# The two matrix products of a feed-forward block take turns on TensorE, one matmul of each

## The chip, the cores and the metric

One NeuronCore of a Trainium2 chip runs the whole program. The metric is the device time of one execution in microseconds (us); less is better. TensorE (PE in the profile) does the matrix products and has a separate row for its weight loads (PEld). VectorE (DVE), ScalarE (ACT) and GpSimd (POOL) do the elementwise work, and SyncE (SP) issues all DMA transfers.

## The reference

Attention over a window of keys and over block summaries comes first, then a feed-forward block with a squared ReLU. Four batches, 8 heads, 768 positions, head size 64; the feed-forward block has 3072 tokens, width 512 and 2048 hidden units.

```python
a = softmax(concat([where(abs(i - j) < 16, s * q @ k.T, -1e9), s * q @ k_sum.T + log(32)]))
x = (a @ concat([v, v_sum])).transpose(0, 2, 1, 3).reshape(3072, 512)
h = x @ w_in                  # 3072 x 2048
g = np.maximum(h, 0.0) ** 2
return (g @ w_out).astype(np.float32)
```

## The kernel before

**Tiling.** The tokens are cut into 48 groups of 64 (`g`), and eight groups make a unit (`u`, 0 to 5) of 512 tokens. The 2048 hidden units are cut into 16 slices (`f`) of 128. A pair (u, f) is an item, and there are 96 items in order. Each product is done in three terms: a high part and a low part of each operand, without low times low (`xh`, `xl` of the input; `gh`, `gl` of the hidden values; two halves of each weight tile `w0_f` and `w1_f`).

**The first product of an item** (task `FI`, function `hidden`, line 676) adds 12 matmuls of 128x512 into one tile `h` of PSUM, of which there are two. ScalarE and VectorE then make `r` (ReLU, task `RL`, line 684), its square (`SQ`, line 690 on VectorE, 686 on ScalarE for the first two units), `gh` (`GH`, line 692) and `gl` (`GL`, line 695).

**The second product of an item** (task `FO`, function `outer`, line 702) is another 12 matmuls, three into each of four tiles `o` that add up over the 16 items of a unit. After the last item of a unit, `put` copies the four tiles (`PC`, line 727 on ScalarE and 729 on VectorE) and stores them (`PS`).

**Attention for later units** runs between: per group, scores (`s`, line 462), on VectorE, ScalarE and GpSimd the softmax, a transposition through memory (`turn`, lines 560 and 566), and the product with the values (`x`, line 578). In a new batch, VectorE also takes maxima over the keys (`kb`, line 310) and sums of the values (`part`, line 389); in the first two batches the means of the values are matmuls (`vps`, line 355). The weights are unpacked once, during unit 0 (`convert`, lines 621 to 644), over a tile `t` from a pool of four that the value loads share.

**The order** is not written by hand. Each step is a task with a cost, a due time and its predecessors. `Plan.order` runs a list scheduler over all engines and emits the tasks in the order in which they start there. The engines then run their queues in that order, each instruction waiting only for its own data. The due time of a second product is 2.5 steps (`LAG` = 2) behind that of its first:

```python
due += (LAG + 0.5) * STEP
todo = [(t, i) for t in range(NTT) for i in range(3)]
if first or last:
    pieces = [[x for x in todo if x[0] == t] for t in range(NTT)]
else:
    pieces = [sorted(todo, key=lambda x: x[1] == 2)]
```

Of the kernel before, what the change touches and what calls it, by code (L numbers as in the profile page):

```python
# [10 lines left out]
F32 = mybir.dt.float32  # L11
F32R = mybir.dt.float32r
U32 = mybir.dt.uint32
I64 = mybir.dt.int64
AF = mybir.ActivationFunctionType
ALU = mybir.AluOpType
# [4 lines left out]
P = 128  # L21
# [5 lines left out]
SQ = 32  # L27
NSQ = P // SQ
UG = 8
TU = UG * TQ  # L30
# [2 lines left out]
NV = 3  # L33
NPE = 16
LAG = 2


REBIAS = 2.0**-112
# [55 lines left out]
class Plan:  # L94
# [8 lines left out]
    def add(self, name, engine, cost, emit, key, after=(), take=(), use=(), size=0, begin=0.0, behind=None):  # L103
        t = Task(name, engine, cost, emit, key, [a for a in after if a is not None], list(take), list(use), size, begin)
        t.behind = behind
        t.index = len(self.tasks)
        self.tasks.append(t)
        for b in t.take + t.use:
            b.users.append(t)
        return t  # L110
# [63 lines left out]
def attention_then_relu2_ffn(  # L174
# [9 lines left out]
    nc = tc.nc  # L184
    B, H, S, D = v.shape
    NT, DM = out.shape
    NF = wW.shape[1]
# [5 lines left out]
    NU = NG // UG  # L193
    KT = DM // P
    NTT = TU // P
# [6 lines left out]
    add = plan.add  # L202
# [3 lines left out]
    def buf(tag, n, shape, dtype, name, pool=None, fixed=False):  # L206
        if tag not in kinds:
            tiles = [cst.tile(list(shape), dtype, name=f"{tag}{i}") for i in range(n)] if fixed else None
            kinds[tag] = Slots(pool or sb, tag, n, tiles)
        assert kinds[tag].n == n  # L210
        return Buf(kinds[tag], shape, dtype, name)

    def o_buf(name, cols=512):
        return buf("o", 4, (P, cols), F32, name, ps)

    def h_buf(name, cols=512):
        return buf("h", 2, (P, cols), F32, name, ps)
# [12 lines left out]
    items = [(u, f) for u in range(NU) for f in range(NF)]  # L230
    T0, SLOW, STEP = 35.0, 7.1, 6.5
    unit_at = [T0 + NF * (SLOW * min(u, 1) + STEP * max(u - 1, 0)) for u in range(NU + 1)]
    at_item = {(u, f): unit_at[u] + f * (STEP if u else SLOW) for u, f in items}
# [18 lines left out]
    xh = cst.tile([P, KT, RING * TQ], F32R, name="xh")  # L252
    xl = cst.tile([P, KT, RING * TQ], F32R, name="xl")
# [45 lines left out]
    t_S, t_KC, t_T, t_V, t_XL = {}, {}, {}, {}, {}  # L299
    t_K = {}  # L300

    def batch_k(b):
        key = wanted(b * NW) - 30 if b else -90
        prev = [t_S[b * NW - 1]] if b else []

        def load(p):
            nc.sync.dma_start(out=kb[:, p, NB:], in_=kT[b, p * P : (p + 1) * P, :])

        def top(p):
            nc.vector.tensor_reduce(  # L310
                out=kb[:, p, :NB], in_=kb[:, p, NB:].rearrange("p (j r) -> p j r", r=BLOCK), op=ALU.max, axis=AX.X
            )

        t_K[b] = []
        for p in range(NPAIR):
            t = add(f"KL{b}_{p}", "SP", 0.45, lambda p=p: load(p), key + 0.1 * p, prev, size=4 * P * S)
            t_K[b].append(add(f"KM{b}_{p}", "DVE", 0.945, lambda p=p: top(p), key + 0.1 * p, [t]))
# [282 lines left out]
    t_W = {}  # L600
    w_bufs = {}

    def convert(f, n):
# [3 lines left out]

        due = at_item[0, f] + (LAG * STEP if n else 0)

# [46 lines left out]
        t_W[n, f] = [t6, t7]  # L656


    t_FI = {}

    def ffn(u, f, o, done):

        first, last = f == 0, f == NF - 1
        due = at_item[u, f]
        c0 = u % 2 * TU
        wi, wo = ([Part(w_bufs[n, f], 0, DM), Part(w_bufs[n, f], DM, 2 * DM)] for n in range(2))
        h = h_buf(f"h{u}_{f}")
        r, gh, gl = (
            buf(tag, n, (P, TU), dt, f"{tag}{u}_{f}") for tag, n, dt in (("r", 2, F32), ("gh", 3, F32R), ("gl", 3, F32R))
        )  # L670

        def hidden():
            i = 0
            for k in range(KT):
                for lhs, rhs in ((wi[0], xh), (wi[1], xh), (wi[0], xl)):
                    nc.tensor.matmul(  # L676
                        h.tile, lhsT=lhs.tile[:, k * P : (k + 1) * P], rhs=rhs[:, k, c0 : c0 + TU],
                        start=(i == 0), stop=(i == 3 * KT - 1),
                    )
                    i += 1  # L680

        deps = t_W[0, f] + [t_XL[g] for g in range(u * UG, (u + 1) * UG)] + list(t_FI.values())[-1:]
        t1 = t_FI[u, f] = add(f"FI{u}_{f}", "PE", 2.79, hidden, due, deps, take=[h])
        t2 = add(f"RL{u}_{f}", "ACT", 0.62, lambda: nc.scalar.activation(r.tile, h.tile, AF.Relu), due + 3, [t1], take=[r], use=[h])  # L684
        if u < 2:
            t3 = add(f"SQ{u}_{f}", "ACT", 0.62, lambda: nc.scalar.activation(r.tile, r.tile, AF.Square), due + 4, [t2], use=[r])
        else:
            t3 = add(
                f"SQ{u}_{f}", "DVE", 0.7,
                lambda: nc.vector.tensor_tensor(out=r.tile, in0=r.tile, in1=r.tile, op=ALU.mult), due + 4, [t2], use=[r],  # L690
            )
        t4 = add(f"GH{u}_{f}", "ACT", 0.62, lambda: nc.scalar.copy(out=gh.tile, in_=r.tile), due + 5, [t3], take=[gh], use=[r])  # L692
        t5 = add(
            f"GL{u}_{f}", "DVE", 0.7,
            lambda: nc.vector.tensor_tensor(out=gl.tile, in0=r.tile, in1=gh.tile.bitcast(F32), op=ALU.subtract),  # L695
            due + 6, [t4], take=[gl], use=[r, gh],
        )
        terms = ((gh, wo[0]), (gh, wo[1]), (gl, wo[0]))

        def outer(todo):  # L700
            for t, i in todo:
                nc.tensor.matmul(  # L702
                    o[t].tile, lhsT=terms[i][0].tile[:, t * P : (t + 1) * P], rhs=terms[i][1].tile,
                    start=(first and i == 0), stop=(last and i == 2),
                )

        due += (LAG + 0.5) * STEP
        todo = [(t, i) for t in range(NTT) for i in range(3)]
        if first or last:
            pieces = [[x for x in todo if x[0] == t] for t in range(NTT)]  # L710
        else:
            pieces = [sorted(todo, key=lambda x: x[1] == 2)]
        for i, piece in enumerate(pieces):
            t6 = add(
                f"FO{u}_{f}_{i}", "PE", 0.2325 * len(piece), lambda piece=piece: outer(piece), due + 0.1 * i,
                [t4, t5] + t_W[1, f] + done[-1:],
                take=[o[i]] if first else [], use=[gh, gl] + ([] if first else [o[i]] if last else o),
            )
            done.append(t6)
            if last:  # L720
                put(u, i, o[i], t6, due + 0.1 * i)

    def put(u, i, o, t, due):
        rows = slice(u * TU + i * P, u * TU + (i + 1) * P)
        x = buf("half", 4, (P, DM), F32, f"os{u}_{i}")
        if i % 2:
            t2 = add(f"PC{u}_{i}", "ACT", 0.62, lambda: nc.scalar.copy(out=x.tile, in_=o.tile), due + 0.6, [t], take=[x], use=[o])
        else:
            t2 = add(f"PC{u}_{i}", "DVE", 0.7, lambda: nc.vector.tensor_copy(out=x.tile, in_=o.tile), due + 0.6, [t], take=[x], use=[o])
        add(f"PS{u}_{i}", "SP", 0.45, lambda: nc.sync.dma_start(out=out[rows, :], in_=x.tile), due + 1, [t2], use=[x], size=4 * P * DM)  # L730
# [6 lines left out]
    def groups(n):  # L737
        nonlocal done_g
        while done_g < n:
            g = done_g  # L740
            b, w = divmod(g, NW)
            if b and not w:
                batch_k(b)
                (batch_v_pe if b < 2 else batch_v)(b)
            attention(g)
            done_g += 1

    groups(UG)
    for f in range(NF):
        for n in range(2):  # L750
            convert(f, n)
    done = []
    for u in range(NU):
        groups((u + 1) * UG)
        o = [o_buf(f"o{u}_{t}") for t in range(NTT)]
        for f in range(NF):
            ffn(u, f, o, done)

    for t in plan.tasks:
        if t.name in FIRST:  # L760
# [51 lines left out]
```

## Time and profile before

| what | value |
|---|---|
| median of 3 runs | 666.93 us (666.03 to 668.0) |
| profiled execution | 667.02 us, span 665.3 us |
| TensorE matmul busy | 643.5 us, 97% of the span, 3544 instructions |
| VectorE / ScalarE / GpSimd busy | 51% / 42% / 13% |
| DMA | 75.61 MB, mean 114 GB/s |

The span is the time between the first and the last instruction of the profiled execution. A row with one start time and a count stands for instructions that follow each other; the recorded time of one matmul is longer than the distance to the next, since they overlap. What a matmul costs in a stream is therefore read from the distance between starts.

### The profile page before, as it was taken

To read this page: it belongs to the slowest core of one execution; us is meant where nothing else is said; L and a number is where in the kernel's file an instruction comes from. 1 tells how busy PE (TensorE), PEld (TensorE's weight loads), DVE (VectorE), ACT (ScalarE), POOL (GpSimd) and SP (SyncE) were. 2 spreads that over 40 slices of the span, in tenths; PEclk is the share of its full clock that TensorE was granted. 3 is DMA by queue.
4 is the path that set the end of the run, shared out by engine and by line. 5 is a ranking of instruction groups with operands and counts; after the bars stand their busy time and mean duration, and the time that the engine had idled before them with its cause. 6 is when DMAs were issued, how large, how long until landed. Compare 5 with 4: busy or idle time off the path is not lost.

```text
span 665.3 us, 9719 instructions
## 1 busy us (share of the span) xinstructions
PE 643.5 (97%) x3544; PEld 511.2 (77%) x3544; DVE 340.3 (51%) x612; ACT 278.6 (42%) x751; POOL 83.6 (13%) x140
## 2 busy tenths in 40 slices
PE   4979999999999999999999999899999999999997
PEld 3557668878887878787888877778878888888886
DVE  4698879985433375644434586443553342322222
ACT  2688559775534443433323432233343242222221
POOL 3741001100201001101110200110110010000000
PEclk9979999999999999999999999999999999999999
DMA  9955657502523381633141482322352311000001
GB/s 308 323 196 180 237 213 245 187 24 75 157 76 80 78 256 42 182 88 76 49 115 45 150 254 75 101 73 75 97 149 56 91 34 33 32 33 1 0 1 63
DMA packets 50215, 75.61 MB, mean 114 GB/s; under 512 B 6440, under 2 KB 22824, under 8 KB 50168
## 3 DMA queue, kind: packets, MB, share of 16 engines
q1 hardware_dynamic: 50168, 75.00, 36.8%
q8 instruction: 28, 0.46, 0.3%
q14 instruction: 19, 0.16, 0.1%
HBM read 59.75 MB, written 14.68 MB: 112 GB/s over the span
## 4 chain that ended last, share of the span: by engine, by line
PE 86%; DVE 4%; SPq 4%; DMA 3%; issue 1%; POOL 1%; ACT 0%; DVEq 0%; ACTq 0%; POOLq 0%
PE h L676 38%; PE o L702 37%; PE s L462 6%; PE x L578 4%; PE vps L355 2%; SPq L560 1%; DMA vr<-v 1%; DVE part L389 1%; DMA fv_lent<-vS 1%; PE t L532 1%; SPq L440 1%; SPq L413 1%; POOL qv_lent L443 0%; DMA a<-turn 0%; DMA out<-os 0%
## 5 line engine op out<-in xcount | busy, mean ns | idle before, releaser
L676 PE MATMUL h<-xh,w 128*128 128x512 f32 x768 | 245.7, 401 | 0.5 <-ACT xh L588 0.5
L702 PE MATMUL o<-w,gh 128*128 128x512 f32 x768 | 203.9, 400 | 0.0
L676 PEld LDWEIGHTS h<-xh,w 128*128 128x128 f32 x768 | 143.2, 189 | 35.0 <-issue 0.8
L702 PEld LDWEIGHTS o<-w,gh 128*128 128x128 f32 x768 | 139.8, 188 | 32.3 <-issue 1.7
L676 PE MATMUL h<-xl,w 128*128 128x512 f32 x384 | 152.8, 398 | 0.3 <-DVE xl L591 0.3
L684 ACT ACTIVATE r<-h 128x512 f32<-128x512 f32 x96 | 57.2, 595 | 183.6 <-PE h L676 159.9
L695 DVE TENSOR_TENSOR gl<-r,gh 128x512 fp32r<-128x512 f32 x96 | 69.1, 720 | 85.4 <-PE o L702 53.8
L702 PE MATMUL o<-w,gl 128*128 128x512 f32 x384 | 109.2, 391 | 0.0
L690 DVE TENSOR_TENSOR r<-r 128x512 f32<-128x512 f32 x64 | 44.8, 700 | 96.8 <-ACT r L684 95.7
L692 ACT CAST gh<-r 128x512 fp32r<-128x512 f32 x96 | 59.6, 621 | 77.7 <-PE o L702 48.9
L676 PEld LDWEIGHTS h<-xl,w 128*128 128x128 f32 x384 | 72.7, 189 | 18.5 <-DVE xl L591 1.0
L702 PEld LDWEIGHTS o<-w,gl 128*128 128x128 f32 x384 | 72.1, 188 | 15.8
L503 ACT ACTIVATE p<-p,nm 128x118 f32<-128x118 f32 x160 | 61.1, 384 | 49.0 <-DVE nm L494 49.0
L519 POOL TENSOR_TENSOR p<-p,nm 128x472 f32<-128x472 f32 x40 | 45.1, 1128 | 184.4 <-DVE nm L513 106.9
L474 POOL COPY kb<-kb 128x96 f32<-128x96 f32 x44 | 17.1, 389 | 275.8 <-PE s L462 271.7
L462 PEld LDWEIGHTS s<-kb,q 128*128 128x128 f32 x320 | 41.6, 191 | 5.2 <-POOL p L483 1.2
L462 PE MATMUL s<-kb,q 128*128 128x118 f32 x320 | 42.1, 274 | 1.0 <-POOL p L483 1.0
L484 DVE SCALAR_TENSOR_TENSOR p<-s,mask 128x472 f32<-128x472 f32 x40 | 25.8, 645 | 26.0 <-PE s L462 25.5
L578 PEld LDWEIGHTS x<-a,v 118*64 118x64 f32 x640 | 22.0, 137 | 17.6 <-issue 12.4
L549 DVE STREAM_TRANSPOSE a<-p 128x512 f32<-128x512 f32 x32 | 22.7, 708 | 19.6 <-POOL p L519 19.6
L512 DVE TENSOR_SCALAR nm<-nm 128x4 f32<-128x4 f32 x48 | 8.9, 185 | 44.9 <-ACT p L503 43.5
L578 PE MATMUL x<-a,v 118*64 118x64 f32 x640 | 27.4, 228 | 3.5 <-DMA a<-turn 2.9
(55 smaller groups left out, 423.3 us busy)
## 6 DMA issues: line engine op xcount, KB each, us to landing
raw<-wW SPq DMA_DIRECT2D x32, 512.0 KB
q<-qW SPq DMA_DIRECT2D x40, 256.0 KB
turn<-a SPq DMA_DIRECT2D x128, 64.0 KB
a<-turn SPq DMA_DIRECT2D x32, 256.0 KB
v<-vS SPq DMA_DIRECT2D x36, 192.0 KB
kb<-kT SPq DMA_DIRECT2D x16, 384.0 KB
out<-os SPq DMA_DIRECT2D x24, 256.0 KB
vr<-v SPq DMA_DIRECT2D x16, 192.0 KB
```

The costliest lines, as they stand in the source:

```text
L462: nc.tensor.matmul(s_ps.tile[:, p * KEYS : (p + 1) * KEYS], lhsT=q.tile[:, p, :], rhs=kb[:, p, k0 : k0 + KEYS], start=True, stop=True,)
L484: nc.vector.scalar_tensor_tensor(out=pr.tile[:, :, :KEYS], in0=s_ps.tile.rearrange("p (n k) -> p n k", k=KEYS), scalar=1.0 / math.sqrt(D), ...
L503: nc.scalar.activation(x, x, AF.Exp, bias=nm.tile[:, p : p + 1], scale=1.0, accum_out=nm.tile[:, NPAIR + p : NPAIR + p + 1],)
L519: nc.gpsimd.tensor_tensor(out=x, in0=x, in1=nm.tile[:, 2 * NPAIR :].unsqueeze(2).broadcast_to([P, NPAIR, KEYS]), op=ALU.mult)
L549: nc.vector.transpose(out=a.tile.rearrange("p (j n r) -> p j n r", j=NSQ, n=NPAIR), in_=pr.tile.rearrange("p n (j c) -> p j n c", c=SQ),)
L578: nc.tensor.matmul(x_ps.tile[h % 2 * D : (h % 2 + 1) * D, h // 2 * TQ : (h // 2 + 1) * TQ], lhsT=vv.tile[:KEYS, h * D : (h + 1) * D], rhs= ...
L676: nc.tensor.matmul(h.tile, lhsT=lhs.tile[:, k * P : (k + 1) * P], rhs=rhs[:, k, c0 : c0 + TU], start=(i == 0), stop=(i == 3 * KT - 1),)
L684: t2 = add(f"RL{u}_{f}", "ACT", 0.62, lambda: nc.scalar.activation(r.tile, h.tile, AF.Relu), due + 3, [t1], take=[r], use=[h])
L690: lambda: nc.vector.tensor_tensor(out=r.tile, in0=r.tile, in1=r.tile, op=ALU.mult), due + 4, [t2], use=[r],
L692: t4 = add(f"GH{u}_{f}", "ACT", 0.62, lambda: nc.scalar.copy(out=gh.tile, in_=r.tile), due + 5, [t3], take=[gh], use=[r])
L695: lambda: nc.vector.tensor_tensor(out=gl.tile, in0=r.tile, in1=gh.tile.bitcast(F32), op=ALU.subtract),
L702: nc.tensor.matmul(o[t].tile, lhsT=terms[i][0].tile[:, t * P : (t + 1) * P], rhs=terms[i][1].tile, start=(first and i == 0), stop=(last an ...
```

## The change

The first and second product are planned together, in one function `ffn(n, done)` for item number n. It cuts the first product of item n into two halves of six matmuls, and also the second product of item n - 2. From item 10 on (`APART`), each half is one task `FM` that emits one matmul of the first product, one of the second, and so on. Ahead of item 10 the halves are tasks of their own. The second product's matmuls are sorted by term, so that neighbours write different `o` tiles; in the first and the last item of a unit they are sorted by pairs of tiles. The elementwise tasks and `put` stay, with due times shifted by 0.4 of a step, and `put` is called for two tiles at a time.

```diff
+APART = 10
...
+            def hidden(k, i):
+                lhs, rhs = ((wi[0], xh), (wi[1], xh), (wi[0], xl))[i]
+                nc.tensor.matmul(
+                    h.tile, lhsT=lhs.tile[:, k * P : (k + 1) * P], rhs=rhs[:, k, c0 : c0 + TU],
+                    start=(k == i == 0), stop=(k == KT - 1 and i == 2),
+                )
+
+            for j in range(3 * KT):
+                parts[2 * j // (3 * KT)][0].append(lambda j=j: hidden(*divmod(j, 3)))
...
+        if n >= LAG:
+            u2, f2 = items[n - LAG]
...
+            todo = [(t, i) for t in range(NTT) for i in range(3)]
+            if first or last:
+                todo.sort(key=lambda x: (x[0] // 2, x[1]))
+            else:
+                todo.sort(key=lambda x: x[1])
+            for j, x in enumerate(todo):
+                parts[2 * j // len(todo)][1].append(lambda x=x: outer(*x))
...
+        def run(*lists):
+            for j in range(max(map(len, lists))):
+                for x in lists:
+                    if j < len(x):
+                        x[j]()
...
+            if n < APART:
+                if first_p:
+                    t = add(f"FI{name}", "PE", 0.2325 * len(first_p), lambda x=first_p: run(x), d, deps[0], take=takes_h, use=uses_h, behind=latest(0))
+                    done[0].append(t)
+                if second_p:
+                    t = add(f"FO{name}", "PE", 0.2325 * len(second_p), lambda x=second_p: run(x), d + 0.5 * STEP, made + t_W[1, f2], take=begun, use=uses[j], behind=latest(1))
+                    done[1].append(t)
+            else:
+                t = add(
+                    f"FM{name}", "PE", 0.2325 * (len(first_p) + len(second_p)), lambda x=first_p, y=second_p: run(x, y), d,
+                    deps[j] + (done[1][-1:] if n == APART else []), take=takes_h + begun, use=uses_h + uses[j],
+                    behind=latest(0),
+                )
+                done[0].append(t)
+                done[1].append(t)
+            if n >= LAG and last:
+                for i in (2 * j, 2 * j + 1):
+                    put(u2, i, o[i], done[1][-1], d + 0.5 * STEP + 0.1 * i)
...
+            due += 0.4 * STEP
...
+    for n in range(len(items) + LAG):
+        if n < len(items) and items[n][1] == 0:
+            groups((items[n][0] + 1) * UG)
+        ffn(n, done)
```

On TensorE, in the middle of unit 2, the queue before has the first product of slice 7 in one piece and then the second product of slice 5 (`h2_7` is the tile of unit 2, slice 7; `o2_0` is output tile 0 of unit 2):

```order
L676 MATMUL h2_7_2897<-xh_68,w0_7_995 128x512 x2
L676 MATMUL h2_7_2897<-xl_69,w0_7_995 128x512
L578 MATMUL x27_2915<-a27_2781,v1_74 64x64 x8
L702 MATMUL o2_0_2687<-w1_5_964,gh2_5_2847 128x512 x2
L702 MATMUL o2_1_2720<-w1_5_964,gh2_5_2847 128x512 x2
L702 MATMUL o2_2_2732<-w1_5_964,gh2_5_2847 128x512 x2
L702 MATMUL o2_3_2749<-w1_5_964,gh2_5_2847 128x512 x2
L702 MATMUL o2_0_2687<-w1_5_964,gl2_5_2849 128x512
L702 MATMUL o2_1_2720<-w1_5_964,gl2_5_2849 128x512
```

At the same place the changed kernel has one matmul of each in turn:

```order
L675 MATMUL h2_7_2883<-xh_68,w0_7_987 128x512
L689 MATMUL o2_0_2607<-w1_5_959,gh2_5_2858 128x512
L675 MATMUL h2_7_2883<-xh_68,w0_7_987 128x512
L689 MATMUL o2_1_2608<-w1_5_959,gh2_5_2858 128x512
L675 MATMUL h2_7_2883<-xl_69,w0_7_987 128x512
L689 MATMUL o2_2_2637<-w1_5_959,gh2_5_2858 128x512
L675 MATMUL h2_7_2883<-xh_68,w0_7_987 128x512
L689 MATMUL o2_3_2638<-w1_5_959,gh2_5_2858 128x512
```

The matmuls are the same; each now has neighbours that write another tile, stream another operand and use other weights.

On ScalarE, in unit 0, the queue before unpacks the weight tile `w1_4` (`t1_4` is its first step) ahead of the exponentials of groups 10 and 11 (`nm10`, `nm11`):

```order
L621 ACTIVATE t1_4_750<-raw1_4_652 128x512
L503 ACTIVATE p0_76,nm10_747<-p0_76,nm10_747 128x118 x4
L692 CAST gh0_3_777<-r0_3_726 128x512
L684 ACTIVATE r0_4_795<-h0_4_754 128x512
L686 ACTIVATE r0_4_795<-r0_4_795 128x512
L641 CAST w1_3_802<-t1_3_691 128x512
L692 CAST gh0_4_813<-r0_4_795 128x512
L539 COPY a10_828<-t10_808 128x4x4x32
L641 CAST w0_5_833<-t0_5_715 128x512
L641 CAST w1_4_852<-t1_4_750 128x512
L621 ACTIVATE t0_6_878<-raw0_6_665 128x512
L503 ACTIVATE p1_77,nm11_876<-p1_77,nm11_876 128x118 x4
```

In the changed kernel the same tile comes behind the exponentials of group 11:

```order
L504 ACTIVATE p1_77,nm11_867<-p1_77,nm11_867 128x118 x4
L622 ACTIVATE t1_4_899<-raw1_4_645 128x512
L750 ACTIVATE r0_5_903<-h0_5_854 128x512
L752 ACTIVATE r0_5_903<-r0_5_903 128x512
L622 ACTIVATE t0_6_914<-raw0_6_660 128x512
L758 CAST gh0_5_919<-r0_5_903 128x512
L642 CAST w1_4_925<-t1_4_899 128x512
```

The first step of `w1_4` moved behind the exponentials of group 11, and its cast also behind the elementwise steps of item 5.

At the end of TensorE's queue, the last item of the last unit was done one output tile after the other:

```order
L702 MATMUL o5_0_5181<-w1_15_1610,gh5_15_5565 128x512 x2
L702 MATMUL o5_0_5181<-w1_15_1610,gl5_15_5567 128x512
L702 MATMUL o5_1_5199<-w1_15_1610,gh5_15_5565 128x512 x2
L702 MATMUL o5_1_5199<-w1_15_1610,gl5_15_5567 128x512
L702 MATMUL o5_2_5203<-w1_15_1610,gh5_15_5565 128x512 x2
L702 MATMUL o5_2_5203<-w1_15_1610,gl5_15_5567 128x512
L702 MATMUL o5_3_5207<-w1_15_1610,gh5_15_5565 128x512 x2
L702 MATMUL o5_3_5207<-w1_15_1610,gl5_15_5567 128x512
```

Now it is done by pairs of tiles:

```order
L689 MATMUL o5_0_5105<-w1_15_1610,gh5_15_5577 128x512
L689 MATMUL o5_1_5106<-w1_15_1610,gh5_15_5577 128x512
L689 MATMUL o5_0_5105<-w1_15_1610,gh5_15_5577 128x512
L689 MATMUL o5_1_5106<-w1_15_1610,gh5_15_5577 128x512
L689 MATMUL o5_0_5105<-w1_15_1610,gl5_15_5579 128x512
L689 MATMUL o5_1_5106<-w1_15_1610,gl5_15_5579 128x512
L689 MATMUL o5_2_5132<-w1_15_1610,gh5_15_5577 128x512
L689 MATMUL o5_3_5133<-w1_15_1610,gh5_15_5577 128x512
```

The first tile is complete two matmuls later than before, the third two later, and the second and fourth where they were.

## Rows read from the trace of the kernel before

**Rows 1.** The page: busy time by engine; granted TensorE clock in 40 slices.

```profile
PE 643.5 (97%) x3544; PEld 511.2 (77%) x3544; DVE 340.3 (51%) x612; ACT 278.6 (42%) x751; POOL 83.6 (13%) x140
...
PEclk9979999999999999999999999999999999999999
```

**Rows 2.** Stretches: us, busy us (instructions) per engine, clock, DMA share, GB/s.

```profile
250.00:300.00 50.00, 49.41 (x272) 40.22 (x273) 27.97 (x48) 18.71 (x55) 6.47 (x9) 1.00 0.36 104
...
400.00:450.00 50.00, 47.09 (x271) 38.07 (x270) 24.69 (x44) 15.65 (x50) 6.01 (x8) 1.00 0.32 83
```

**Rows 3.** Groups of TensorE, 60 to 660 us: busy, mean ns, idle before, releasers.

```profile
L578 PE MATMUL x<-a,v 118*64 118x64 f32 x624 | 26.7, 228 | 3.5 <-DMA a<-turn 2.9 <-DMA out<-os 0.6
```

**Rows 4.** Chain that ended last, 570 us to the end: start, us, what.

```profile
575.49 0.69 PE o L702 x3
...
608.90 2.81 PE h L676 x12
611.71 2.76 PE o L702 x12
...
645.12 16.50 PE o L702 x72
...
661.63 0.59 ACT os L727
```

**Rows 5.** Timeline of TensorE, 581 to 594 us: start, recorded us, instruction.

```profile
582.07 0.40 PE L676 MATMUL h<-xl,w 128*128 128x512 f32 x1
582.31 0.63 PE L702 MATMUL o<-w,gh 128*128 128x512 f32 x2
582.78 0.39 PE L702 MATMUL o<-w,gl 128*128 128x512 f32 x1
583.01 0.63 PE L676 MATMUL h<-xh,w 128*128 128x512 f32 x2
...
585.59 0.39 PE L676 MATMUL h<-xl,w 128*128 128x512 f32 x1
585.82 0.62 PE L702 MATMUL o<-w,gh 128*128 128x512 f32 x2
```

**Rows 6.** Timeline of TensorE, 603 to 612 us.

```profile
607.83 1.07 PE L702 MATMUL o<-w,gl 128*128 128x512 f32 x4
608.74 0.63 PE L676 MATMUL h<-xh,w 128*128 128x512 f32 x2
```

**Rows 7.** Timeline, 66 to 92 us, of four engines in unit 0.

```profile
79.96 0.63 ACT L686 ACTIVATE r<-r 128x512 f32<-128x512 f32 x1
80.62 0.62 ACT L692 CAST gh<-r 128x512 fp32r<-128x512 f32 x1
...
82.48 1.04 PE L355 MATMUL vps<-fv,means 128*24 128x512 f32 x2
...
83.45 2.11 PE L702 MATMUL o<-w,gh 128*128 128x512 f32 x8
```

**Rows 8.** Timeline, 385 to 430 us: ScalarE and VectorE at the start of a batch.

```profile
389.65 3.52 DVE L310 TENSOR_REDUCE kb<-kb 128x24 f32<-128x768 f32 x4
...
389.83 0.60 ACT L684 ACTIVATE r<-h 128x512 f32<-128x512 f32 x1 [1.74 <-DVE gl L695]
...
393.09 3.22 DVE L389 TENSOR_REDUCE part<-vr 96x64 f32<-96x512 f32 x3
...
397.58 0.68 DVE L690 TENSOR_TENSOR r<-r 128x512 f32<-128x512 f32 x1
...
398.50 0.62 ACT L692 CAST gh<-r 128x512 fp32r<-128x512 f32 x1
```

**Rows 9.** DMA, 655 to 666 us, in 40 slices: busy tenths, GB/s.

```profile
DMA  0000000000000000000000799999999930000000
GB/s 0 0 0 0 0 0 0 0 0 0 0 0 0 0 0 0 0 0 0 0 0 0 268 372 380 410 365 358 372 380 380 387 142 0 0 0 0 0 0 0
```

More of the change, by code (lines that the diff above doesn't have):

```diff
@@ L656, in convert @@
         t_W[n, f] = [t6, t7]
[L659 to L701, printed above, removed]
@@ new lines, in attention_then_relu2_ffn, with ffn, outer @@
+    t_FI, second = {}, {}
+    def ffn(n, done):
+        parts = [([], [], []), ([], [], [])]
+        deps, uses = [[], []], [[], []]
+        if n < len(items):
+            u, f = items[n]
+            c0 = u % 2 * TU
+            wi = [Part(w_bufs[0, f], 0, DM), Part(w_bufs[0, f], DM, 2 * DM)]
+            h = h_buf(f"h{u}_{f}")
+            def hidden(k, i):
[6 more added lines that the diff above has]
+                parts[2 * j // (3 * KT)][0].append(lambda j=j: hidden(*divmod(j, 3)))
+            deps[0] += t_W[0, f] + [t_XL[g] for g in range(u * UG, (u + 1) * UG)]
+        if n >= LAG:
+            u2, f2 = items[n - LAG]
+            first, last = f2 == 0, f2 == NF - 1
+            o, terms, made, bufs = second[n - LAG]
+            def outer(t, i):
@@ L705, in outer @@
                 )
[L707 to L717, printed above, removed]
-            )
-            done.append(t6)
-            if last:
-                put(u, i, o[i], t6, due + 0.1 * i)
+            todo = [(t, i) for t in range(NTT) for i in range(3)]
@@ new lines, in ffn @@
+            if first or last:
[4 more added lines that the diff above has]
+                parts[2 * j // len(todo)][1].append(lambda x=x: outer(*x))
+            for j in range(2):
+                deps[j] += made + t_W[1, f2]
+                uses[j] += bufs
+                if first:
+                    parts[j][2].extend(o[2 * j : 2 * j + 2])
+                else:
+                    uses[j] += o[2 * j : 2 * j + 2] if last else o
@@ new lines, in latest @@
+        def latest(i):
+            return done[i][-1] if done[i] else None
+        def run(*lists):
[3 more added lines that the diff above has]
+                        x[j]()
+        due = at_item[items[n]] if n < len(items) else at_item[items[-1]] + STEP * (n - len(items) + 1)
+        for j, (first_p, second_p, begun) in enumerate(parts):
+            takes_h = [h] if first_p and j == 0 else []
+            uses_h = [h] if first_p and j else []
+            d = due + 0.5 * STEP * j
+            name = f"{n}_{j}"
+            if n < APART:
[5 more added lines that the diff above has]
+                    done[1].append(t)
+            else:
+                t = add(
[8 more added lines that the diff above has]
+                    put(u2, i, o[i], done[1][-1], d + 0.5 * STEP + 0.1 * i)
@@ new lines, in ffn @@
+        if n < len(items):
+            t1 = t_FI[u, f] = done[0][-1]
+            wo = [Part(w_bufs[1, f], 0, DM), Part(w_bufs[1, f], DM, 2 * DM)]
+            r, gh, gl = (
+                buf(tag, nb, (P, TU), dt, f"{tag}{u}_{f}") for tag, nb, dt in (("r", 2, F32), ("gh", 3, F32R), ("gl", 3, F32R))
+            )
+            due += 0.4 * STEP
+            t2 = add(f"RL{u}_{f}", "ACT", 0.62, lambda: nc.scalar.activation(r.tile, h.tile, AF.Relu), due + 3, [t1], take=[r], use=[h])
+            if u < 2:
+                t3 = add(f"SQ{u}_{f}", "ACT", 0.62, lambda: nc.scalar.activation(r.tile, r.tile, AF.Square), due + 4, [t2], use=[r])
+            else:
+                t3 = add(
+                    f"SQ{u}_{f}", "DVE", 0.7,
+                    lambda: nc.vector.tensor_tensor(out=r.tile, in0=r.tile, in1=r.tile, op=ALU.mult), due + 4, [t2], use=[r],
+                )
+            t4 = add(f"GH{u}_{f}", "ACT", 0.62, lambda: nc.scalar.copy(out=gh.tile, in_=r.tile), due + 5, [t3], take=[gh], use=[r])
+            t5 = add(
+                f"GL{u}_{f}", "DVE", 0.7,
+                lambda: nc.vector.tensor_tensor(out=gl.tile, in0=r.tile, in1=gh.tile.bitcast(F32), op=ALU.subtract),
+                due + 6, [t4], take=[gl], use=[r, gh],
+            )
+            if f == 0:
+                os_bufs[u] = [o_buf(f"o{u}_{t}") for t in range(NTT)]
+            second[n] = os_bufs[u], ((gh, wo[0]), (gh, wo[1]), (gl, wo[0])), [t4, t5], [gh, gl]
@@ L723, in put @@
+    os_bufs = {}
     def put(u, i, o, t, due):
@@ L751, in attention_then_relu2_ffn @@
             convert(f, n)
[L752 to L757, printed above, removed]
+    done = [], []
+    for n in range(len(items) + LAG):
+        if n < len(items) and items[n][1] == 0:
+            groups((items[n][0] + 1) * UG)
+        ffn(n, done)
     for t in plan.tasks:
```

## Prediction

> **What bounds the kernel now.** [...] Busy time of overlapping matmuls doesn't prove a full engine, so the stretches come next: from 50 us on they show no idle time on TensorE but for 0.59 us between 250 and 300 us and 2.91 us between 400 and 450 us [rows 2]. The groups say what that is: all 3.5 us stand ahead of the value matmuls `x`, and nearly all of it was ended by a DMA, the transposed weights of attention coming back from memory [rows 3]. So the kernel is a queue of TensorE work, and two things can change its time: what one matmul costs in its place in the queue, and a new hole in the queue. No matmul is added or removed.
>
> What one costs is read in the chain near the end, where nothing else runs: 12 matmuls of a first product take 2.81 us, 0.2342 each, and 12 of a second product 2.76 us, 0.230 each [rows 4].
>
> **The rate of the turns.** From item 10 to item 95, 86 items take turns: 86 x 12 = 1032 pairs, one of each product, which now cost 0.2342 + 0.230 = 0.4642 us.
>
> If writing the same PSUM tile twice in a row cost something, taking turns would gain it. A first product writes one tile 12 times in a row, and its matmuls are the dearer ones. But the second product has its own test: the last item of a unit does three matmuls in a row into one tile, in 0.69 us, 0.230 each, and the last 72 matmuls, most of which are done as two into one tile and then the next, take 16.50 us, 0.229 each [rows 4]. So the same tile again costs nothing that these rows show.
>
> The crossings from one product to the other are what the changed kernel consists of. From a first product's last matmul to the start of a second product's first there are 0.24 and 0.23 us, mean 0.235; from a second product's last to a first product's first, 0.23 [rows 5]. These are steps from one tile, one streamed operand and one weight source to another. The cost stays with the matmul that streams, whichever follows. A pair at these two is 0.465 us, 0.0008 more than now, or **+0.8 us** over 1032 pairs. The rows are rounded to 0.01 us, so this is known to some 0.01 us per pair only. The bounds: the cheapest stream in the trace is the low term of the second product, where four neighbours write four tiles, at 0.91 us for four, 0.2275 each [rows 6]; two of these make 0.455 a pair, -9.5 us in all. The dearest is the 0.24 crossing [rows 5] with 0.234 behind it, +10 us. I take the crossings, since they are the same steps, and keep both ends.
>
> [...]
>
> **Unit 0.** Items 0 to 9 don't take turns but are re-ordered. On ScalarE the weight tile `w1_4` now starts behind the exponentials of group 11, and its cast stands behind ReLU, square, another unpacking and `gh` of item 5, so that it ends five ScalarE steps after the first product of item 5 does. Such steps take 0.62 to 0.63 us [rows 7], so 3.1 us. TensorE has in that time two `vps` matmuls (0.97 us from 82.48 to 83.45 [rows 7]) and six of a second product (1.38 us), 2.35 us in all, and then wants `w1_4`. It waits 0.75 us, with hand-overs about **+1.0 us**. TensorE has no holes behind this that could take the loss back [rows 2]. Before, the tile was early enough: the second product at 83.45 follows the `vps` pair directly [rows 7]. Bounds: 0, if the exponentials come earlier, and +2.5 us, if the low half of the tile (a cast and two VectorE steps of some 0.7 later) is what is waited for.
>
> **The holes of 3.5 us.** They hang on how far `x` of a group stands behind its scores in the queue and on what SP and VectorE have in front of the transposition. The order of all of these is made anew by the planner, so neither their staying nor their going follows from a row of before. I take half, **-1.75 us**, with 0 and -3.5 us as bounds.
>
> **The end.** The last four stores move 1.05 MB and keep the DMA engines busy without a break at 358 to 410 GB/s [rows 9]; what sets the end is when the first of them starts. The first output tile is complete two matmuls later, 2 x 0.23 = **+0.45 us**. Bounds: 0, if the last copy (661.63 us, 0.59 us [rows 4]) sets the end, and +0.7 us, a whole store.
>
> **The lag.** In the turns, a second product follows its first by exactly one item (24 matmuls, 5.57 us, with a score or value group some 6.4 us), where the planner was free before. ReLU, square and `gh`, 0.6 to 0.7 us each [rows 7, 8], take 2 us when nothing holds them. They are costed at nothing, with that cover; the second rival is the case without it.
>
> **Sum** against the profiled execution's own 667.02 us, which is 0.09 us above the median of three runs: +0.8 + 1.0 - 1.75 + 0.45 = +0.5, **667.5 us**. A measurement of this kernel can tell about 0.3%, 2.0 us, from no change, so the forecast is no change that can be seen.
>
> **The rivals.** *A cheaper rate, faster.* All turns go at the 0.2275 us of the low terms: -9.5 + 1.0 - 1.75 + 0.45 = -9.8, 657.2 us. For it speaks that these are the only rows where every neighbour writes another tile; against it, that four neighbours there also stream the same operand, which the turns never do, and that a first product's cost doesn't fall at its last matmul. [...]
>
> *The holes go, and nothing is lost, faster.* -3.5 + 0.8 + 0.45 = -2.25, 664.8 us; the order of `w1_4` speaks against it. Chance 0.11.
>
> *The lag is too short, slower.* At the start of batch 3 VectorE has maxima of 3.52 us and sums of 3.22 us in a row, and between them an item's ReLU at 389.83 waits until 397.58 for its square and until 399.12 for the end of `gh` [rows 8]: 9.3 us. With a cover of 6.4 us TensorE would stand for 2.9 us, in batch 2 likewise, since from unit 2 on the square is VectorE's: +5.8 us, with the other terms 673.3 us. It decides from 6.4 us on; at 7.4 us in both places it is just seen. Against it speaks that the planner knows the shorter lag and may put the square ahead of the sums. Chance 0.17.
>
> *Unit 0 loses more and the holes stay, slower.* +2.5 + 0.8 + 0.45 = +3.75, 670.8 us. Chance 0.10.
>
> **How the numbers follow.** The forecast has 0.42 and is the likeliest; its own range is 665 to 669 us. Faster: 0.20 + 0.11 = 0.31; the same 0.42; slower 0.17 + 0.10 = 0.27. The range for 8 in 10 takes in the cheaper rate at 657.2 and the short lag at 673.3 us, and leaves out both ends of the rate where they go further: 657 to 674 us.
>
> **What would show it.** In the profile after, 24 matmuls of an item in turns take 5.57 us in the chain, and 24 first-to-second steps 0.235 and 0.23 us in the timeline; 5.46 us would show the cheaper rate. A wait of TensorE ahead of `o` in unit 0 near 84 us, released by ScalarE's cast of `w`, shows the loss there. Idle time ahead of `x` after 250 us shows what became of the holes, and idle time ahead of `o`, released by `gh` on ScalarE near 290 and 400 us, the short lag. The span ended 3.7 us behind the last matmul (665.3 against 645.12 + 16.50); 4.1 us shows the later stores. The prediction is wrong if the rate of the turns differs from the sum of its two parts by over 0.002 us a pair, since 1032 pairs make 2 us of that.

## The result and the profile after

The changed kernel takes 667.9 us (median of 20 runs, 665.6 to 669.9), the kernel before 666.6 us (20 runs). The ratio is 1.0024, 95% interval 1.0014 to 1.0035: a loss that can just be told from none, and less than the 0.3% that the prediction counted as a change. The profiled execution took 666.66 us with a span of 665.0 us, against 667.02 and 665.3 us before. So the two profiles don't show the loss in their sums; they show terms of both signs, and one of these, the start, is not the change's.

The page of the changed kernel, busy time and granted clock, as in [rows 1]:

```profile
PE 644.9 (97%) x3544; PEld 510.0 (77%) x3544; DVE 339.5 (51%) x612; ACT 279.1 (42%) x751; POOL 82.3 (12%) x140
...
PEclk9989999999999999999999999999999999999999
```

The stretches of [rows 2], same columns:

```profile
250.00:300.00 50.00, 50.00 (x280) 40.42 (x277) 25.84 (x46) 19.13 (x56) 5.54 (x8) 1.00 0.37 103
400.00:450.00 50.00, 49.59 (x281) 39.91 (x280) 25.65 (x47) 16.79 (x51) 5.82 (x8) 1.00 0.34 88
```

The groups of TensorE from 60 to 660 us, as in [rows 3]:

```profile
L463 PE MATMUL s<-kb,q 128*128 128x118 f32 x296 | 39.1, 275 | 0.4 <-POOL kb L475 0.4
L579 PE MATMUL x<-a,v 118*64 118x64 f32 x624 | 26.7, 228 | 0.0
```

The 3.5 us ahead of `x` are gone, 0.4 us ahead of a score group `s` have come, and the matmuls of both products (`h`, `o`) wait for nothing. That full queue still takes as long, so its matmuls must have become dearer. The timeline of TensorE shows how: here stands the first matmul of each second product in unit 5, so that from row to row there are 24 matmuls of an item.

```profile
588.27 0.39 PE L689 MATMUL o<-w,gh 128*128 128x512 f32 x1
...
593.79 0.39 PE L689 MATMUL o<-w,gh 128*128 128x512 f32 x1
...
599.32 0.39 PE L689 MATMUL o<-w,gh 128*128 128x512 f32 x1
...
604.98 0.39 PE L689 MATMUL o<-w,gh 128*128 128x512 f32 x1
...
610.50 0.39 PE L689 MATMUL o<-w,gh 128*128 128x512 f32 x1
```

The items take 5.52, 5.53, 5.66 and 5.52 us, where an item took 5.57 before [rows 4]. The dear one is that with slice 6 of the first product, and the pace changes at its border within one step. Over units 1 to 5 (mean distance from one start to the next, steps under 0.26 us) a first product's matmul costs 232.4 ns and a second's 232.8 ns, 465.2 ns a pair against 463.3 before. By slices of the first product, a pair costs 469 to 473 ns for slices 0, 1, 6, 14 and 15, 464 for 9 to 13, and 460 to 462 for the other six, in all five units alike. In the kernel before the slices range from 461 to 466 ns, without this pattern.

### The profile page after: what moved, and what is told of

Same layout as the page of the kernel before. It is cut to its first block, busy times and chain, and to the rows that moved or that the text cites. A ratio compares the mean times of both kernels' runs of the same rounds, so it can differ in the third digit from the quotient of the medians.

```text
span 665.0 us, 9704 instructions
## 1 busy us (share of the span) xinstructions
PE 644.9 (97%) x3544; PEld 510.0 (77%) x3544; DVE 339.5 (51%) x612; ACT 279.1 (42%) x751; POOL 82.3 (12%) x140
## 4 chain that ended last, share of the span: by engine, by line
PE 94%; DVE 3%; DMA 1%; POOL 1%; ACT 0%; issue 0%; SPq 0%; POOLq 0%
PE h L675 41%; PE o L689 40%; PE s L463 6%; PE x L579 4%; PE vps L356 2%; DMA kb<-kT 1%; PE t L533 1%; DVE raw L625 1%; POOL qv_lent L444 0%; DVE t L631 0%; DVE t L637 0%; DVE nm L495 0%; DVE xl L592 0%; DVE w L645 0%; ACT p L504 0%
## 5 line engine op out<-in xcount | busy, mean ns | idle before, releaser
L675 PE MATMUL h<-xh,w 128*128 128x512 f32 x768 | 304.7, 405 | 0.7 <-ACT xh L589 0.7
L689 PE MATMUL o<-w,gh 128*128 128x512 f32 x768 | 294.0, 396 | 0.0
L689 PEld LDWEIGHTS o<-w,gh 128*128 128x128 f32 x768 | 143.4, 188 | 33.9 <-issue 2.5
L750 ACT ACTIVATE r<-h 128x512 f32<-128x512 f32 x96 | 57.1, 595 | 227.4 <-PE h L675 227.4
L689 PE MATMUL o<-w,gl 128*128 128x512 f32 x384 | 146.8, 394 | 0.0
L761 DVE TENSOR_TENSOR gl<-r,gh 128x512 fp32r<-128x512 f32 x96 | 65.5, 683 | 40.8 <-ACT gh L758 40.6
L475 POOL COPY kb<-kb 128x96 f32<-128x96 f32 x44 | 14.9, 340 | 282.2 <-PE s L463 282.2
L504 ACT ACTIVATION_READ_ACCUMULATOR p<-p,nm 128x1 f32 x160 | 30.0, 188 | 0.0
L513 DVE TENSOR_SCALAR nm<-nm 128x4 f32<-128x4 f32 x48 | 8.9, 185 | 40.7 <-ACT p L504 39.1
```

Of the source, the lines that this page charges most:

```text
L504: nc.scalar.activation(x, x, AF.Exp, bias=nm.tile[:, p : p + 1], scale=1.0, accum_out=nm.tile[:, NPAIR + p : NPAIR + p + 1],)
L675: nc.tensor.matmul(h.tile, lhsT=lhs.tile[:, k * P : (k + 1) * P], rhs=rhs[:, k, c0 : c0 + TU], start=(k == i == 0), stop=(k == KT - 1 and ...
L689: nc.tensor.matmul(o[t].tile, lhsT=terms[i][0].tile[:, t * P : (t + 1) * P], rhs=terms[i][1].tile, start=(first and i == 0), stop=(last an ...
```

## The experiments

Twelve kernels ran. Rates are means over units 1 to 5, as above.

**Blocks in the new plan (no_turns).** In the function that emits a half:

```diff
-            for j in range(max(map(len, lists))):
-                for x in lists:
-                    if j < len(x):
-                        x[j]()
+            for x in lists:
+                for y in x:
+                    y()
```

> The changed plan in halves stays, but from item 10 on a half emits its six matmuls of the first product and then its six of the second, in place of one of each in turn. Theory (the turns themselves cost about 2 ns a pair, and the new plan does the rest): spacing goes back to some 233.5 ns for a first product's matmul and 229.5 to 230 for a second's, 463.3 ns a pair in place of 465.3; 1032 pairs make 2.1 us, so 666.0 us against 667.9 of the changed kernel and 666.6 of before, a ratio to before of about 0.999. Units without holes (1 and 5) get shorter by 0.35 us each against the changed kernel, and there is still no idle time ahead of the value matmuls after 250 us, since the plan is the same. Rival (turning costs nothing, the difference sits in the plan): within 0.5 us of the changed kernel, ratio 1.002.

Measured: 666.98 us, ratio 1.0013 (1.0001 to 1.0025), 464.8 ns a pair; unit 1 takes 102.93 us against 103.03, unit 5 94.48 against 94.62; 0.4 us of idle time ahead of `x`. The theory fell half: taken as a mean, the turns cost 0.4 ns a pair, and 1.5 ns come with what this kernel keeps of the change, the new plan with its blocks of six sorted by term (the second product's matmuls went from 229.7 to 231.1 ns); these were not parted. That the holes went with the plan and not with the turns held, but for 0.4 of 3.5 us.

**Where the weights lie (w0_low, w0_high, before_w0_low).** A mean of 465.2 hides slices at 460 and at 473 ns. The slices' weight tiles lie at addresses that the order of first use hands out. These kernels claim the places up front, in another order; instructions and plan are the same. For w0_low and, in the kernel before, before_w0_low:

```diff
+    for x in [f"w{n}_{f}" for n in (0, 1) for f in range(NF)]:
+        sb.tile([P, 2 * DM], F32, tag=x, name=f"{x}_at", bufs=1)
```

w0_high has `for n in (1, 0)`. The expectations draw a line at byte 114688 of a partition and call what lies below it the lower half. In w0_low and before_w0_low the first weights of slices 0 to 12 lie below the line, those of slices 14 and 15 and all second weights above it.

> [...] Plan and instructions are the same. Theory (in turns, a matmul whose neighbour loads a first weight from the lower half goes slower): slices 0 to 12 go at 235 ns for the first product's step and 238 for the second's, 473 ns a pair; slices 14 and 15 at 231 and 230, 461 ns; mean about 471, 6 us more than the changed kernel, 674 us, ratio to before about 1.011. Rival (what differs from slice to slice hangs on the slice, its PSUM bank or its place in the order, not on the address): slices 0, 1, 6, 14, 15 stay the dear ones and the time is that of the changed kernel, ratio 1.002.

> The changed kernel with its tiles only placed anew in SBUF: all first weights above byte 114688, the second weights of slices 0 to 12 below it. Theory: no slow slice is left; first product's step 231 ns, second's 232.8 (230 for slices 14 and 15 of the second weights), 463.5 ns a pair, 1.8 ns less than in the changed kernel, 1.9 us in all: 666.0 us, ratio to before about 0.999. Rival (the address plays no part): the rates by slice and the time of the changed kernel, ratio 1.002.

> The kernel before with the placement of w0_low: first weights of slices 0 to 12 in the lower half, all second weights in the upper. Theory (the price hangs on the turns: in blocks of 12 a first weight is loaded while a first product's own operand streams, and the spacing there didn't differ between slices in the lower and the upper half): no slice differs by over 1 ns, the time is that of before, ratio 1.000 within 0.001. Rival (a first weight in the lower half costs its neighbour whatever the order): first product's steps of slices 0 to 12 go from 233.5 to 238 ns or more, 12 x 13 x 6 steps by 4 ns, 4 us more, ratio 1.006.

Measured: w0_low 673.65 us, ratio 1.0119 (1.0102 to 1.0136); w0_high 673.96 us, 1.0120 (1.0104 to 1.0136); before_w0_low 665.43 us, 0.9990 (0.9977 to 1.0004). w0_low met its number, but not its reason: slices 14 and 15, in the upper half, went at 473.2 and 471.3 ns like the rest, and w0_high, which should have been fast, shows the same rates slice by slice. The halves of SBUF are refuted as the cause in these kernels, and so is the rival that it is the slice. Placement alone made 6 us in turns (673.65 us against the changed kernel's 667.9) and, in blocks, nothing that can be told from the time (ratio 0.9990). The windows of 570 to 640 us, where TensorE runs the two products alone, show it in one number, the instructions on TensorE (behind the first x). The kernel before, the changed kernel, then w0_low, then w0_high:

```profile
570.00:640.00 70.00, 70.00 (x303) 56.66 (x302) 19.20 (x28) 16.92 (x28) 0.00 (x0) 1.00 0.04 15
```

```profile
570.00:640.00 70.00, 70.00 (x304) 56.64 (x303) 18.62 (x27) 16.84 (x28) 0.00 (x0) 1.00 0.04 16
```

```profile
570.00:640.00 70.00, 70.00 (x297) 55.66 (x296) 18.61 (x27) 16.52 (x28) 0.00 (x0) 1.00 0.04 16
```

```profile
570.00:640.00 70.00, 70.00 (x297) 55.63 (x296) 17.92 (x26) 15.69 (x26) 0.00 (x0) 1.00 0.04 16
```

The granted clock is 1.00, the full level, in all four, and the engine is never idle: 70 us for 303 and 304 or for 297 matmuls.

**The offset (w_at160, gh_at2016, w_at0, before_w_at160).** What the slow slices of the changed kernel share is the place of the first weights within 2048 bytes: 2016, and 160 for the fast ones (three small tiles of 64 bytes lie between the two kinds). `gh` and `gl` lie at 160. In w0_low and w0_high all weights lie at 2016. In the code `w0` is the weight operand (`lhsT`) of a first product and `xh` or `xl` the streamed one; of a second product, `gh` or `gl` and `w1`. The trace of the changed kernel has one weight load of 128x128 for each matmul, 189 ns in a first product and 188 in a second (means), and in turns they alternate between the two products. The edits are pads around the weights of w0_low, here that of w_at160:

```diff
+    sb.tile([P, 48], F32, tag="pad0", name="pad0", bufs=1)
     for x in [f"w{n}_{f}" for n in (0, 1) for f in range(NF)]:
         sb.tile([P, 2 * DM], F32, tag=x, name=f"{x}_at", bufs=1)
+    sb.tile([P, 464], F32, tag="pad1", name="pad1", bufs=1)
```

> The halves of SBUF fell as a cause: with the first weights low or high the same slices went at the same 470 to 473 ns a pair. What the slow slices share is their offset: 2016 bytes past a multiple of 2048, while the fast ones stand 160 bytes past one. This kernel is w0_low with a pad of 192 bytes ahead of the weights and one of 1856 behind them: all weights at offset 160, gh and gl at offset 160 as before. Theory (the offset of a weight tile sets the pace of the turns): every slice goes at the 460 to 461 ns a pair that the changed kernel shows for slices 2 to 5, 12 ns less than w0_low, so 12 us less than its 673.7: 661.5 to 663.5 us, ratio to before 0.993 to 0.996. Rival (the offset is a chance likeness, and what counts is the distance of the two weight tiles or the half together with something else): 470 to 473 ns a pair stay, ratio 1.012.

> w0_low with a pad of 1856 bytes behind the weights alone: weights stay at offset 2016, gh and gl move from 160 to 2016. It parts two forms of the theory. Own offset (a weight at 2016 is slow to load or to stream, whatever the others have): 471 to 473 ns a pair as in w0_low, ratio 1.012 or more. Same offset (first weight and gh, which are loaded in turn, are fast where they have one offset): 460 to 461 ns, ratio 0.993 to 0.996.

> w0_low with 32 bytes ahead of the weights and 2016 behind them: weights at offset 0, gh and gl at 160. Own offset, in the form that crossing a boundary of a power of two costs: at offset 0 no slice of 512 bytes crosses one of 512 to 2048, so 461 ns a pair or less, ratio 0.996 or less. Same offset: weights and gh differ, so 470 ns or more, ratio 1.010 or more.

> The kernel before with the placement of w_at160. Theory (the offset has a price in turns alone, since in blocks of 12 the slices at 160 and at 2016 went alike): 463.3 ns a pair and the time of before, ratio 1.000 within 0.001. Rival (the offset matters in blocks too): some 2 ns or more less a pair, ratio 0.997 or less.

Measured: w_at160 662.77 us, ratio 0.9955 (0.9938 to 0.9973), 460.5 ns a pair, no slice beyond 461.3. gh_at2016 663.61 us, 0.9967 (0.9954 to 0.9981), 461.2 ns. w_at0 665.99 us, 1.0007 (0.9994 to 1.0020), 463.3 ns in every slice. before_w_at160 666.49 us, 1.0003 (0.9989 to 1.0017), 463.9 ns. So weights at 2016 go at 471.5 ns a pair with `gh` at 160 (w0_low) and at 461.2 with `gh` at 2016 (`r` and other tiles moved with `gh` and `gl`, but the two products read none of them): between these kernels it is the distance that counts, not the place of either. w_at0 went between what both theories said: neither fast nor slow. The windows of w_at160 and gh_at2016:

```profile
570.00:640.00 70.00, 70.00 (x306) 57.01 (x305) 18.37 (x27) 16.19 (x27) 0.00 (x0) 1.00 0.04 16
```

```profile
570.00:640.00 70.00, 70.00 (x306) 57.19 (x305) 19.34 (x28) 16.89 (x28) 0.00 (x0) 1.00 0.04 16
```

**The period (w_off_128, w_off_512, w_off_64).** w_at160 with the first pad larger by so many bytes and the second smaller.

> w_at160 with the weights 128 bytes further (320 bytes of pad ahead, 1728 behind): offset 288 against 160 of gh and gl. It asks for the period of the rule that the same offset is fast. Differences known: 0 goes at 460.5 ns a pair, 160 less than gh at 463.3, 1856 more than gh (192 less than a multiple of 2048) at 471.5. If the period is 128 bytes, 460.5 ns as in w_at160; if it is longer, dearer than 463 ns.

> w_at160 with the weights 512 bytes further (704 bytes of pad ahead, 1344 behind): offset 672 against 160. If the period is 512 bytes or a part of it, 460.5 ns a pair; if it is 1024 or 2048, dearer than 463 ns.

> w_at160 with the weights 64 bytes further (256 bytes of pad ahead, 1792 behind): offset 224 against 160 of gh and gl. Distances of 128 and 512 bytes went as fast as none, 460.4 and 461.1 ns a pair, 160 (32 more than 128) at 463.3, and the slow one, 1856, is 64 more than 14 times 128. If the rule is one of 128 bytes, 64 is the worst distance: 471 to 473 ns a pair, the time of w0_low, ratio to before about 1.012. If the slow case hung on 2016 itself, 460 to 463 ns and a ratio of 0.996 to 1.000.

Measured: w_off_128 461.2 ns a pair (one run, 663.0 us); w_off_512 460.5 ns (one run, 664.7 us, its first product 1.9 us later than in w_at160); w_off_64 471.5 ns, 673.21 us, ratio 1.0102 (1.0085 to 1.0119). So 128 and 512 bytes off went like none (460.5 ns in w_at160), and 64 off did not. Taken modulo 128, the distance of the weights from `gh` and `gl` orders all placements here that have one distance for all slices: at 0 they take 460.5 to 461.2 ns (these two, w_at160 and gh_at2016), at 32 463.3 (w_at0, the only kernel at it), at 64 471.5 (three kernels). No other distance was run. The window of w_off_64, whose plan and instructions are those of w_at160 and whose weights alone lie 64 bytes further:

```profile
570.00:640.00 70.00, 70.00 (x298) 55.63 (x297) 18.61 (x27) 16.59 (x28) 0.00 (x0) 1.00 0.04 16
```

**Unit 0 and the end (whole_tail).** w_at160 with two edits:

```diff
-            if first or last:
+            if first:
                 todo.sort(key=lambda x: (x[0] // 2, x[1]))
-            else:
+            elif not last:
                 todo.sort(key=lambda x: x[1])
...
+        if n < APART:
+            parts = [tuple(a + b for a, b in zip(*parts))]
+            uses[0] = uses[0] + [b for b in uses[1] if b not in uses[0]]
```

> w_at160 with two edits in other stretches: ahead of item 10 an item's products are planned whole, not in halves, and the last item of a unit is done tile by tile as in the kernel before. Theory: the 1.1 us that unit 0 lost came with the halves (more steps from one kind of matmul to another), so unit 0 goes from 110.2 back to about 109.2 us; the end (last matmul to end of span) goes from 3.7 to 3.1 us. Together 1.5 us less than w_at160: some 661.3 us, ratio to before 0.993 to 0.994. Rival (unit 0's loss sits in the shifted due times and not in the halves): unit 0 stays at 110.2 us, and the sum is 0.5 us less than w_at160.

Measured: 662.25 us, ratio 0.9929 (0.9912 to 0.9946), the lowest median of this study, though its interval overlaps that of w_at160. Unit 0 takes 109.24 us in place of 110.18, as expected: the halves were the cause. The three kernels in the old plan take 109.0 to 109.6 us there, the ten with halves 110.1 to 111.2, so the step is larger than the scatter. The end gained nothing: the span ends 4.3 us behind the last matmul's end, as in the changed kernel. (The expected 3.7 and 3.1 us are in fact the times from the end of the last copy to the end of the span, in the changed kernel and in the kernel before.) The timeline shows where the gain went; of whole_tail:

```profile
654.41 0.69 DVE L784 COPY os<-o 128x512 f32<-128x512 f32 x1 [0.91 <-PE o L694]
...
655.09 0.59 ACT L782 COPY os<-o 128x512 f32<-128x512 f32 x1 [2.31 <-PE o L694]
...
655.71 2.19 SPq L785 DMA_DIRECT2D out<-os  x4
```

Tile 0 is copied by 655.10, and yet the first store goes out at 655.71, when tile 1's copy on ScalarE ends. The queue of SP has them that way round, and so it is in the changed kernel, shown here:

```
L777 DMA out<-os5_1_5595 128x512
L777 DMA out<-os5_0_5593 128x512
```

As the code has it, the planner lets both copies start at the same instant, since both hang on one task, and counts 0.62 for ScalarE's and 0.70 for VectorE's; so it expects tile 1 first. No kernel had the two stores the other way round.

## Why the prediction was right

The forecast of no visible change, 667.5 us, held against 667.9, as did its own range of 665 to 669. Its terms did less well, and two of its reasons failed.

**The rate of the turns: the sign was right, the size was not, and the claim behind it was wrong.** Forecast +0.8 us; measured 465.2 less 463.3 ns, over 1032 pairs +2.0 us. Most of the miss is in the pair of before: the prediction took 464.2 ns from one item near the end, and over units 1 to 5 it is 463.3, 0.9 us in all. The pair in turns was met, 465 against 465.2 ns. By the prediction's own sign of being wrong, a rate over 2 ns a pair off the sum of its parts, the mean just passes at 1.9 ns; the five slow slices, at 6 to 10 ns, don't.

Of the 1.9 ns the turns themselves are 0.4 (no_turns to the changed kernel) in this placement. "The cost stays with the matmul that streams, whichever follows" is refuted: between w_at160 and w0_low the same 2064 matmuls in the same order differ by 11 ns a pair, and from w0_low to gh_at2016 a first product's matmul goes from 235.1 to 231.9 ns though none of its own tiles moved. None of it was to be seen by slices in the kernel before (461 to 466 ns, without the pattern), where the weights lie at the same addresses. The crossings of [rows 5] were the right steps, and their mean over units 1 to 5 is 465.0 ns a pair too, but here the crossings among blocks didn't show what placement made of a stream of crossings: with all weights 64 bytes off they come to 467.8 ns a pair (before_w0_low) and turns cost 471.5, with none off to 462.7 (before_w_at160) and turns cost 460.5.

The two bounds, -9.5 and +10 us, held what placement alone made of it: 460.5 ns is -2.9 us against before, 471.5 is +8.5 us. The rate came out near the forecast because the placement by chance mixes five slow slices, five in between and six fast: that is luck. The 0.20 in the sum of the chances for faster is that of the first rival, the cheaper rate of 455 ns a pair for all turns, or of a rate below it. It was nearest in w_at160, with 460.5 ns a pair, 230.3 a matmul; no run shows a lower mean of pairs in turns.

**Unit 0: right size, wrong place.** Forecast +1.0 us from a wait for `w1_4`; measured 110.25 less 109.14, +1.1 us, from first product to first product, but that wait is not there. Timeline of the changed kernel, 78 to 88 us:

```profile
81.84 1.04 PE L356 MATMUL vps<-fv,means 128*24 128x512 f32 x2
...
82.81 0.73 PE L689 MATMUL o<-w,gh 128*128 128x512 f32 x2
...
84.18 0.61 ACT L642 CAST w<-t 128x512 fp32r<-128x512 f32 x1
84.38 1.04 PE L356 MATMUL vps<-fv,means 128*24 128x512 f32 x2
85.35 1.66 PE L689 MATMUL o<-w,gh 128*128 128x512 f32 x6
```

The cast came as late as predicted, done at 84.79, 2.95 us behind the first product of item 5. But TensorE had 3.51 us of work, not 2.35: a second pair of `vps` (84.38) stands in the queue that the working left out. The halves cost it instead (whole_tail gives 0.93 us back). One step of it can be pointed at: between the values and a transposition there are now eight score matmuls and six of a first product, where there were twelve of a first product, and TensorE waits ahead of the transposition.

```profile
56.11 0.63 PE L533 MATMUL t<-ident,p 128*128 128x128 f32 x4 [0.36 <-DVE xl L592]
```

The kernel before and whole_tail have no such wait from 51 to 68 us. Where the other 0.6 us or so lie was not settled.

**The holes: forecast -1.75, measured -3.1 us** in the two profiles (3.5 ahead of `x` [rows 3] against 0.0, and 0.4 ahead of `s`). That half would stay was a guess, and all ahead of `x` went; no_turns, with 0.4 us ahead of `x` and 0.4 ahead of `s`, shows that they went with the plan. Their size varies from profile to profile: the two other kernels in the old plan have 1.8 (before_w0_low) and 2.6 us (before_w_at160) ahead of `x`, and all eleven in the new plan 0.4 to 1.0 us ahead of `x` and `s` together. The means, 2.6 and 0.8 us, make the change -1.9 us, near the guess. The rows of before_w0_low and of before_w_at160, as in [rows 3]:

```profile
L581 PE MATMUL x<-a,v 118*64 118x64 f32 x624 | 26.7, 228 | 1.8 <-DVE r L693 1.4 <-DMA a<-turn 0.4
```

```profile
L583 PE MATMUL x<-a,v 118*64 118x64 f32 x624 | 26.7, 228 | 2.6 <-DMA a<-turn 2.1 <-DMA out<-os 0.5
```

**The end: forecast +0.45, measured +0.6 us** (4.30 us from the last matmul's end to the end of the span, 3.72 before), most of it for the reason given. The first tile is complete two matmuls later, and then its store waits for another tile's copy. Of the changed kernel:

```profile
659.09 0.69 DVE L776 COPY os<-o 128x512 f32<-128x512 f32 x1 [1.37 <-PE o L689]
...
659.31 0.59 ACT L774 COPY os<-o 128x512 f32<-128x512 f32 x1 [2.32 <-PE o L689]
...
659.92 2.20 SPq L777 DMA_DIRECT2D out<-os  x4
```

Of the kernel before:

```profile
659.58 0.69 DVE L729 COPY os<-o 128x512 f32<-128x512 f32 x1 [5.42 <-PE o L702]
...
660.29 2.28 SPq L730 DMA_DIRECT2D out<-os  x4
```

Before, the first store went out 0.02 us behind the first copy, 1.31 us ahead of the last matmul's end; now 0.14 us behind it and 0.73 ahead. From the first store to the end of the span it is 5.0 us in both and in whole_tail. So 0.45 us are the later tile, as forecast, and some 0.12 the wait for the other copy. In whole_tail the first copy is as early as before, but the store waits 0.61 us behind it: the second reason grew by what the first gave back. That the order of the two stores is what has to change follows from these rows and was not run.

**The lag** cost nothing, as forecast: 0.0 us of idle time ahead of `o`.

**The sum.** With the sizes of the two profiles it is +2.0 + 1.1 - 3.1 + 0.6 = +0.6 us, against +0.5 forecast: errors of +1.2, +0.1, -1.35 and +0.15 that cancelled, which is luck. With the mean holes of all kernels it is +1.8 us. The timed difference of the medians, +1.3 us, lies between. The profiled execution shows -0.36 us because its first product started 1.0 us earlier behind the first matmul (38.1 against 39.1 us), which the other runs put at 37.5 to 39.4 us without pattern.

## What to carry to other kernels

When two streams of matmuls are interleaved, read the price of a pair slice by slice. Here it couldn't be read from the few crossings of the blocked order (465.0 ns, where turns took 460.5 to 471.5 by placement), and not from one mean either (465.2, by slices 460 to 473); the pace that changed at a tile's border and repeated in all five units went with the tiles' places. Then look at the offsets of the weight tiles that are loaded in turn, and try a pad of some bytes before judging the order: here the same interleaving is 1.0% slower (w_off_64) or 0.5% faster (w_at160) than blocks by 64 bytes of it. And where a step of a queue is costed by its cover, list every instruction of that cover from the order itself; the missed `vps` pair undid a wait that was otherwise computed right.

## What was not expected of the hardware

In turns, at a granted clock of 1.00, a pair of 128x512 matmuls took 460.5 to 461.2 ns where the two kinds of weight tiles (`w0` with `w1`, and `gh` with `gl`) lie a multiple of 128 bytes apart (w_at160, gh_at2016, w_off_128, w_off_512), 463.3 ns at 32 bytes off (w_at0) and 471.5 at 64 (w0_low, w0_high, w_off_64). In blocks of twelve, where neighbours load from one tile, moving the weights from 64 to 0 made no difference that can be told from the time (ratios 0.9990 and 1.0003 to before). Only the steps from one product to the other change tiles there, and in these two kernels they differ: from first to second and back they take 237.4 and 230.4 ns at 64 (before_w0_low), 235.3 and 227.4 at 0 (before_w_at160), 5 ns per item, too little to be seen in the time. Within a block all loads lie a multiple of 128 bytes apart, and a pair costs 463.3 ns (the kernel before) and 463.9 (before_w_at160) all the same, so the distance is not all that made the rate. In the changed kernel, slices whose streamed `w1` alone is 64 off pay 3.5 ns (464), and the one whose loaded `w0` alone is off (slice 6) pays 11 to 12 (472), which points to the two tiles that are loaded as weights in turn for most of the price. The reason was not shown: `xh` and `xl` stayed at offset 0 throughout, and no kernel moved them, or `w0` without `w1`, by itself.
